# Swapping the partition halves of landmark sums by DMA instead of folding them on TensorE, with a new start and new schedule constants

## Chip, cores, metric

One core of one Trainium2 chip. The metric is the device time of one execution in microseconds (us), the slowest core's. Executions of one kernel mostly agree within 0.3%, though here runs of the kernel before lie between 252.5 and 256.1 us. Every comparison below is therefore with runs of the kernel before on the same chip, in the same rounds.

A ratio is the mean time of one kernel's fast runs over the mean time of the other's fast runs of the same rounds, so it isn't quite the ratio of the medians that are quoted. "Span" is the time from the first to the last instruction in a profiled run, some 1.7 to 2.1 us less than that run's time. "First MLP matmul" is always the first product of group `ps<-AT,G`, and not the product with w_in that comes before it.

## The reference

Nyström attention on 8 batches, 8 heads, 576 tokens, head size 64, then an MLP with squared relu. Landmarks are means of 18 neighbouring tokens of q and of k; 32 for each head.

```python
q_lm = q.reshape(B, H, m, S // m, D).mean(axis=3)      # m = 32
k_lm = k.reshape(B, H, m, S // m, D).mean(axis=3)
A  = sm(q, k_lm);  Bm = sm(q_lm, k_lm);  C = sm(q_lm, k)
Z = Bm.T / (norm1(Bm) * norm_inf(Bm) + 1e-06)
for _ in range(6):
    Z = 2 * Z - Z @ Bm @ Z
x = (A @ Z @ C @ v)             # heads side by side: (4608, 512)
g = np.maximum(x @ moe_w_in, 0.0) ** 2                  # (4608, 2048)
out = g @ moe_w_out
```

## The kernel before

A list scheduler inside the kernel (`Plan`) orders all operations when the program is built. It has a cost for each operation and a table of small moves (`SHIFTS`, one byte for each operation), searched offline for exactly this list of operations. On the chip each engine then runs its operations in that fixed order and waits where data is late.

The code cuts of this document are shortened. For batches 2 to 7 VectorE makes the landmark sums from the transposed q and k. The transposed tiles hold the 64 head dimensions of even tokens in one half of the partitions and those of odd tokens in the other, so each landmark is split into two partial sums, one in each half. A matmul with a fold matrix adds the halves, and the result has to come out of PSUM again:

```python
# attention(b), sums by VectorE
s1: t1 = T[:, :, 0, :] + T[:, :, 1, :]
s2: t2 = t1 + T[:, :, 2, :]
s3: part = reduce_sum(t2)                      # 128 partitions x 256, two halves to be added
...
def fold_mm(e, part=part, fp=fp):
    t = bank(fp, [P, H, M])
    nc.tensor.matmul(t.rearrange("p h m -> p (h m)"), lhsT=fold[:], rhs=part, start=True, stop=True)
...
if nm == "k":
    add(either(256), ... copy(e, kdup[:], PS[fp][:]), reads=[fp], writes=["kdup"])
else:
    for i in range(2):
        add(either(256), ... copy(e, bdq[64 * i:64 * i + 64, :, i, :], PS[fp][64 * i:64 * i + 64, :, :]), ...)

def b_mm(e):                                   # the landmark product, first user of kdup
    ...
    nc.tensor.matmul(t[:, i, :], lhsT=qpad[:, P * h:P * h + P], rhs=kdup[:, h, :], ...)
```

The start of batch 0: half of k comes in f32 through SyncE's queue and is cast by the engines, half by GpSimd's casting load. TensorE warms up with 46 zero matmuls, then transposes k in two groups of 12 chunks.

```python
def stage_k(e):
    nc.sync.dma_start(kst..., k[0, 0:H // 2]...)
...
load("k", 0, 2, (1,))                          # heads 4 to 7, casting
...
n = 12 if first else 6                         # chunks in a group of transposes
fill = {("k", 0): 46, ("q", 0): 3}.get((nm, x0), 0) if first else 0
```

The next batch's input loads are issued by GpSimd as soon as the transposes of the batch at hand have landed: a copy of one element of `qT` to `gate` makes GpSimd wait for them.

The softmax here doesn't subtract the row's maximum and nothing guards it: scores larger than these inputs give would overflow.

## Time and profile before

| | before |
|---|---|
| median of three runs | 254.35 us (254.19 to 254.66) |
| span of the profiled run, a fourth one of 253.56 us | 251.9 us |
| TensorE busy from 30 to 248 us | 214.92 of 218 us |
| first matmul of the MLP | 23.14 us |

The landmark product, first user of the folded sums, in the groups of instructions; the columns are line, engine, operation, tiles, sizes and count, then busy time in us and mean ns, then idle time before them with what ended it:

```profile
L707 PE MATMUL ps<-kdup,qpad 128*128 128x32 bf16 x56 | 2.5, 176 | 0.0
```

TensorE waits 0.0 us for it: kdup is always there in time. Two stretches in which the changed kernel will turn out differently (length, then PE, PEld, DVE, ACT, POOL, granted clock, DMA share, GB/s):

```profile
65.00:70.00 5.00, 4.95 (x56) 3.06 (x55) 4.22 (x14) 3.98 (x9) 0.00 (x0) 1.00 1.12 201
92.00:102.00 10.00, 9.79 (x129) 5.95 (x130) 9.12 (x34) 7.46 (x13) 0.18 (x1) 1.00 0.88 152
```

TensorE is full in both, at full clock.

### The profile page before, as it was taken

The page shows a single profiled execution, that of the slowest core. Times are in us where ns is not written, and L with a number is a line of the kernel's source. Part 1 is how long each engine was busy: PE and PEld are TensorE (multiplying, and loading weights), DVE is VectorE, ACT ScalarE, POOL GpSimd, SP SyncE. Part 2 cuts the span into 40 slices and gives each one's busy share as a digit, 9 for nine tenths or more (in the row PEclk, how much of TensorE's full clock was granted, in tenths as well). Part 3 has the DMA queues.
Part 4 walks back from the last instruction along what each step waited for, and adds up shares of the span by engine and source line. Part 5 has one row for each costly group of instructions (what it writes and reads, how often), then busy time and mean ns, then how long its engine had stood idle before and what let it go on. Part 6 is the DMA issues. An engine that isn't in the chain of part 4 may idle for free.

```text
span 251.9 us, 6505 instructions
## 1 busy us (share of the span) xinstructions
PE 240.2 (95%) x2621; PEld 144.5 (57%) x2658; DVE 173.1 (69%) x479; ACT 164.7 (65%) x287; POOL 28.9 (11%) x51
## 2 busy tenths in 40 slices
PE   7887999999999999999999999999999999999993
PEld 7563874557554665466646565556544664466453
DVE  3664887869874999499698797987932756477000
ACT  3386898068773997487879977667814873388021
POOL 7822200004004000300220003001000000000000
PEclk9997999999999999999999999999999999999999
DMA  7999999999998999799599778999222203211123
GB/s 151 186 204 205 205 206 205 189 180 159 217 168 165 187 178 183 109 215 158 119 151 249 135 149 111 222 174 162 72 61 75 57 18 86 61 34 32 42 83 85
DMA packets 57054, 35.58 MB, mean 141 GB/s; under 512 B 29760, under 2 KB 52544, under 8 KB 57024
## 3 DMA queue, kind: packets, MB, share of 16 engines
q0 software_dynamic: 22672, 18.06, 48.0%
q1 hardware_dynamic: 34352, 17.11, 32.3%
q8 instruction: 20, 0.33, 0.5%
q14 instruction: 10, 0.08, 0.1%
HBM read 36.70 MB, written 9.44 MB: 183 GB/s over the span
## 4 chain that ended last, share of the span: by engine, by line
PE 84%; DMA 6%; issue 2%; POOL 2%; ACT 2%; DVE 1%; SPq 0%; ACTq 0%; POOLq 0%; DVEq 0%
PE ps L1179 47%; PE ps L380 13%; PE ps L1123 12%; DMA vraw<-in_v_dram 4%; PE ps L1061 3%; DMA out_dram<-o 3%; PE ps L917 2%; PE ps L966 1%; PE ps L869 1%; PE ps L899 1%; PE ps L1006 1%; PE ps L681 1%; POOL qraw L456 1%; DVE gT L1138 1%; PE ps L948 0%
## 5 line engine op out<-in xcount | busy, mean ns | idle before, releaser
L1179 PE MATMUL ps<-w_out_bf,gT 128*128 128x512 bf16 (+1 forms) x557 | 137.7, 373 | 2.1 <-issue 1.0
L1135 ACT ACTIVATE r<-ps 128x576 bf16<-128x576 f32 x128 | 76.5, 661 | 12.1 <-PE ps L380 10.5
L1179 PEld LDWEIGHTS <-gT 128*128 128x128 bf16 x592 | 53.5, 98 | 46.2 <-issue 5.7
L1138 DVE TENSOR_TENSOR gT<-r 128x576 bf16<-128x576 bf16 x128 | 55.9, 454 | 17.5 <-PE ps L1179 8.6
L1123 PE MATMUL ps<-AT,G 128*128 128x288 bf16 x256 | 66.5, 288 | 0.4
L380 PE MATMUL ps<-AT,G 128*128 128x288 bf16 x256 | 66.5, 288 | 0.0
L388 ACT COPY o<-ps 128x512 f32<-128x512 f32 (+1 forms) x30 | 17.1, 572 | 42.0 <-PE ps L1179 35.6
L380 PEld LDWEIGHTS <-G 128*128 128x128 bf16 x256 | 25.2, 98 | 10.6 <-issue 0.2
L1123 PEld LDWEIGHTS <-G 128*128 128x128 bf16 x256 | 25.2, 98 | 9.8 <-ACT G L388 0.8
L388 ACT CAST G<-ps 128x1024 bf16<-128x1024 f32 (+2 forms) x22 | 19.5, 940 | 5.2 <-PE ps L1061 5.1
L390 DVE CAST G<-ps 128x1024 bf16<-128x1024 f32 (+2 forms) x14 | 14.9, 1070 | 8.3 <-PE ps L1061 8.1
L882 DVE SCALAR_TENSOR_TENSOR st<-st,ps 128x128 bf16<-128x128 bf16 x35 | 10.0, 286 | 10.8 <-PE ps L869 10.7
L553 POOL COPY gate<-qT 1x1 bf16<-1x1 bf16 x6 | 1.6, 274 | 126.6 <-DMA qT<-qraw 107.6
L924 ACT ACTIVATE EC<-ps 96x512 bf16<-96x512 f32 x24 | 13.2, 605 | 0.5 <-PE ps L917 0.5
L532 DVE TENSOR_TENSOR Pd<-st,ones_d 128x256 bf16<-128x256 bf16 x42 | 12.2, 290 | 0.9
L869 PEld LDWEIGHTS <-Pd 128*128 128x128 bf16 x84 | 7.8, 97 | 8.5 <-DVE Pd L532 1.7
L1011 ACT ACTIVATE Ra<-ps 128x576 f32<-128x576 f32 x16 | 10.4, 655 | 3.5 <-PE ps L380 3.3
L1022 DVE TENSOR_TENSOR AT<-Ea,Ra 128x576 bf16<-128x576 bf16 x16 | 11.8, 753 | 0.3 <-ACT Ra L1015 0.3
L999 ACT ACTIVATE Ea<-ps 128x576 bf16<-128x576 f32 x16 | 9.8, 653 | 2.6 <-PE ps L899 2.5
L1061 PE MATMUL ps<-w_in_bf,WT 64*32 64x512 bf16 (+1 forms) x264 | 10.6, 390 | 0.0
L560 PE MATMUL ps<-zeros 128*128 128x128 bf16 (+2 forms) x51 | 6.2, 295 | 2.5 <-DVE zeros L482 1.3
L917 PEld LDWEIGHTS <-kT 128*128 128x128 bf16 x192 | 7.3, 98 | 2.0 <-DMA out_dram<-o 0.6
(156 smaller groups left out, 247.8 us busy)
## 6 DMA issues: line engine op xcount, KB each, us to landing
vraw<-in_v_dram POOLq DMA_DIRECT2D x8, 576.0 KB, 7.9
out_dram<-o SPq DMA_DIRECT2D x23, 192.0 KB, 2.7
qraw<-in_q_dram POOLq DMA_DIRECT2D x7, 576.0 KB, 13.4
kraw<-in_k_dram POOLq DMA_DIRECT2D x7, 576.0 KB, 11.0
out_dram<-o SPq DMA_DIRECT2D x24, 128.0 KB, 2.4
w_in_bf<-in_moe_w_in_dram POOLq DMA_DIRECT2D x4, 512.0 KB, 14.7
w_out_bf<-in_moe_w_out_dram POOLq DMA_DIRECT2D x4, 512.0 KB, 21.0
out_dram<-o SPq DMA_DIRECT2D x23, 64.0 KB, 2.6
```

The costliest lines, as they stand in the source:

```text
L380: nc.tensor.add_instruction(mybir.InstMatmult(start_tensor_calc=start, stop_tensor_calc=stop, is_transpose=transpose, ldweights=False, til ...
L388: nc.scalar.copy(dst, src)
L390: ENG[e].tensor_copy(dst, src)
L532: nc.vector.tensor_tensor(dst[:], src.unsqueeze(2).to_broadcast([P, 2, NG, M]), ones_d[:].unsqueeze(1).to_broadcast([P, 2, NG, M]), ALU.mult)
L917: nc.tensor.matmul(t[:, y, :], lhsT=Ts["k"][z][:, o:o + P], rhs=flat(bdq[:, h, :, :]), start=True, stop=True)
L924: nc.scalar.activation(EC[:, x, :, :, :, :].rearrange("p c i g m -> p (i g) c m"), PS[sc][0:TP, :, :].rearrange("p y (c m) -> p y c m", c= ...
L1022: add(("DVE", dve_ns(S)), lambda e, i=i: nc.vector.tensor_tensor(AT[:, i, :], Ea[:, i, :, :].rearrange("p c t -> p (c t)"), Ra[:, i, :, :] ...
L1061: nc.tensor.matmul(ts[i][M * g:M * g + M, lo:hi], lhsT=WT[64 * i:64 * i + 64, g, :], rhs=w_in_bf[64 * i:64 * i + 64, g, n * 512 + lo:n * 5 ...
L1123: (again if j else nc.tensor.matmul)(t[:, j, 0:HALF], lhsT=G[:, i, f * P:(f + 1) * P], rhs=AT[:, i, j * HALF:(j + 1) * HALF], start=(i == ...
L1135: add(("ACT", act_ns(S)), lambda e, hk=hk, r=r: nc.scalar.activation(r.rearrange("p (j t) -> p j t", j=2), PS[hk][:, :, 0:HALF], AF.Relu), ...
L1138: add(("DVE", dve_ns(S, 2)), lambda e, r=r, f=f: nc.vector.tensor_tensor(gT[:, f, z * S:z * S + S], r[:], r[:], ALU.mult), reads=[("r", rn ...
L1179: nc.tensor.matmul(PS[ok][:, 0:hi - lo], lhsT=gT[:, f, x0:x0 + P], rhs=w_out_bf[:, f, lo:hi], start=(f == f0), stop=(f == f1 - 1))
```

## The change

The intent is to take 12 fold matmuls and 18 PSUM evictions off the engines. A DMA by SyncE copies each half of the partial sums into the other half of a second tile, and VectorE adds the two tiles in bf16. Beside that the start is changed (two heads of k in f32, six by the casting load, finer transposes, more filling matmuls), and the scheduler gets other constants for loads and instruction fetch, with a new table of moves. The core of the diff (the table, declarations and repeated lines cut):

```diff
-LOADS = {11: 1.0, 12: -1.0, 14: 1.0, 15: -1.0, 20: 2.0, 22: -2.0}
+LOADS = {11: 1.0, 12: -1.0, 13: 1.0, 14: -1.0, 21: 1.0, 22: -1.0}
 SHIFTS = ( ... )                                   # new table, cut
-    DMA_NS_PER_BYTE = 1.0 / 410.0
+    DMA_NS_PER_BYTE = 1.0 / 401.0
-    ... FETCH = 256, 67, ((20000.0, 6000.0), ...
+    ... FETCH = 256, 67, ((22000.0, 6400.0), ...
+            if op.dma < 0:
+                op.fin = op.end + op.land
-                op.fin = dma_free + (650.0 if op.lead > 0 else 4500.0)
+                op.fin = dma_free + op.land         # 1200 for loads; first k and q loads times 1.11
...
+    qpart = sb.tile([P, NG, 2, M], BF16, name="qpart")
+    swaps = {nm: sb.tile([P, NG, 2, M], BF16, name=nm + "sw") for nm in ("k", "q")}
-    kst = sb.tile([TP, H // 2, NC6 * D], F32, name="kst")
+    kst = sb.tile([TP, 2, NC6 * D], F32, name="kst")
...
-                n = 12 if first else 6
+                n = 6 if fine else 12               # fine: all but q of batch 0
-                    fill = {("k", 0): 46, ("q", 0): 3}...
+                    fill = {("k", 0): 60, ("q", 0): 3}...
+                        if n == 6:
+                            idle(bank(tp, [P, 512]))   # up to 8 zero matmuls before the second group of k
...
+            if b > 1:
+                def swap(e, part=raw_part[nm], sw=swaps[nm]):
+                    for x in range(2):
+                        nc.sync.dma_start(sw[64 * x:64 * x + 64], part[64 - 64 * x:P - 64 * x])
+
+                add(("SP", 120.0), swap, ..., dma=-1.0, prio=-40.0 + b, land=3500.0)
+                if nm == "k":
+                    add(("DVE", ...), ... tensor_tensor(kdup..., parts["k"][:], swaps["k"][:], ALU.add), ...)
+                else:
+                    add({"POOL": 500.0}, ... tensor_copy(parts["q"], qpart[:]), ... writes=["qpad"])
+                    for i in range(2):
+                        add(("DVE", ...), ... tensor_tensor(bdq[r, :, i, :]..., qpart[r], swaps["q"][r], ALU.add), ...)
+                continue
...
-            cuts = [(0, 256), (256, 512)] if last else [(0, 512)]
+            cuts = [(0, 384), (384, 512)] if last else [(0, 512)]
...
-                          k[0, 0:H // 2]...
+                          k[0, 0:2]...
-    load("k", 0, 2, (1,))
+    add(("POOL", 475.0), lambda e: nc.gpsimd.dma_start(raws["k"][0][:, 2:H], k[0, 2:H]...), ...)
```

`land=3500.0`: the scheduler assumes that a swap lands 3.5 us after its issue.

## The prediction

> **What bounds the kernel now.** I read the page's first two parts, then busy time by stretches, then the chain that ended last in order of time, then the TensorE timeline around the operations that the change takes away, then the transfers. Page, busy time and the clock of 40 slices:
>
> ```profile
> PE 240.2 (95%) x2621; PEld 144.5 (57%) x2658; DVE 173.1 (69%) x479; ACT 164.7 (65%) x287; POOL 28.9 (11%) x51
> ...
> PEclk9997999999999999999999999999999999999999
> ...
> q8 instruction: 20, 0.33, 0.5%
> ```
>
> Busy time by stretches (length, then PE, PEld, DVE, ACT, POOL, granted clock, DMA share, GB/s):
>
> ```profile
> 0.00:10.00 10.00, 8.13 (x121) 7.07 (x122) 5.22 (x23) 2.67 (x5) 8.50 (x21) 1.00 0.90 161
> 10.00:20.00 10.00, 7.98 (x229) 5.48 (x230) 5.69 (x29) 7.87 (x19) 3.99 (x6) 1.00 1.27 202
> 20.00:30.00 10.00, 9.13 (x133) 6.18 (x134) 6.59 (x16) 7.35 (x16) 2.52 (x4) 0.83 1.27 206
> 30.00:248.00 218.00, 214.92 (x2144) 125.80 (x2175) 155.63 (x413) 146.44 (x250) 13.92 (x22) 1.00 0.77 136
> ```
>
> From 30 to 248 us TensorE is busy 214.92 of 218 us. There time is saved only by giving TensorE less to do, or by removing part of 3.1 us of gaps. The rest is the start (the first matmul of the MLP is issued at 23.14 us) and the tail. The start, from the chain in order of time (start, length, what):
>
> ```profile
> 6.61 9.83 DMA vraw<-in_v_dram
> 16.48 1.19 PE ps L948 x24
> ...
> 18.98 0.24 DVE Z4T L983
> 19.26 0.32 PE ps L560
> 19.98 0.75 issue
> ...
> 130.80 6.52 DMA out_dram<-o
> ```
>
> The first batch's v lands at 16.44 us; from it a fixed chain runs to the MLP. In that chain 0.75 us is "issue", in the middle of one group of equal small matmuls, so no data was awaited. The clock was 0.83 on average between 20 and 30 us: one stretch of 3.4 us at half speed (the row of stretches for 22.00 to 25.40 has 0.50). MLP matmuls of 288 columns are 0.24 us apart there, 0.12 us later.
>
> The operation that the change removes, in the TensorE timeline:
>
> ```profile
> 32.28 0.27 PE L681 MATMUL ps<-kpart,fold 128*128 128x256 bf16 x1
> 32.38 0.27 PE L681 MATMUL ps<-qpad,fold 128*128 128x256 bf16 x1
> 32.49 0.29 PE L1123 MATMUL ps<-AT,G 128*128 128x288 bf16 x1
> ```
>
> Starts are 0.10 and 0.11 us apart: this, not the 0.27 us of its length, is what a fold costs a saturated TensorE.
>
> **What the Trainium skill says.** "TensorE: Matmul & The Clock Gate", section Back-to-back issue gap, gives N/2.4 + 2.5 ns warm, 109 ns for 256 columns; the trace agrees (0.21 us for two). The same page, "The HAM clock gate", tells of half speed for a window of some 3.4 us after too little activity; the trace agrees, with one such window in mid-run. "Runtime: NRT & Kernel Launch", section Instruction fetch mechanics: instructions come in blocks of 16 KiB, 256 instructions, at a cost that is mostly hidden. The trace has 20 such packets of 16 KB, and one is not hidden: the 0.75 us above. "DMA: Bandwidth & Descriptors", section Queues, rings and completion order, says that an engine goes round between its queues a packet at a time. The trace is harsher on a late comer: with input loads in flight a store takes 5 to 7.7 us to land, against 2.0 to 2.4 us when it is alone.
>
> **The change part by part.**
>
> 1. Folds. Landmark sums lie as partial sums in two halves of the partitions; a matmul with a fold matrix added the halves. For the six batches 2 to 7 both folds (k, q) go: 12 x 0.108 us = 1.3 us off TensorE, in its saturated stretch. Batches 0 and 1 keep theirs. With them go 6 k evictions (386 ns ACT or 421 ns DVE) and 12 q evictions (368 or 421 ns). In their place: 24 transfers of 32 KB by SyncE, 18 bf16 additions on VectorE, and 6 copies on GpSimd (sums into the padded q). An addition of 256 columns in bf16 should take what the mask multiplication of that size takes in the group list, 290 ns. Per batch VectorE gets 3 x 0.29 = 0.87 us and loses about half of three evictions, 0.6 us: +0.3 us; ScalarE loses about 0.6 us. Neither bounds the whole, so no gain beyond the 1.3 us.
>
> 2. The wait in its place. A swap issued alone should land after 2.0 to 2.3 us. But the next batch's loads are issued as soon as q's transpose lands: 57.4 us for v, the last landing near 70 us. VectorE ends the k sums at 60.97 us and the q sums at 65.47 us, in the midst of it. From the stores in that state I estimate 4.5 to 5.5 us for a swap; the plan in the code allows 3.5. In the changed program's order VectorE does the whole of the q sums, some squares and other work between the k sums and the k addition: 7 squares x 0.45 + 2 x 0.55 + 0.95 = 5.2 us in batch 2, 3.9 us in batch 3. So the k swap is nearly hidden. Between the q sums and the q additions lie 3.4 to 4.6 us of work, plus the landmark exponential in some batches: VectorE may stand for 0 to 1.5 us per batch. Four buffers between ScalarE and VectorE and three score banks pass little of that to TensorE: I book 0.4 us in all.
>
> 3. Mode switches. Going between full and split array costs about 0.09 us in the trace (0.309 us instead of 0.216 between a 512-column matmul and the next kind). In the built order after the first MLP matmul there are 58 such switches before and 55 after: 0.3 us less.
>
> 4. The start. SyncE now brings 2 heads of k in f32 instead of 4, GpSimd's cast load 6 instead of 4. The f32 part had landed at 5.14 us and should land near 3.8. But source bytes ahead of v are the same 4.6 MB and the DMA engines have been busy from 2 us on, so v lands at 16.4 to 16.8 us as before. The warm-up goes from 46 to 60 zero matmuls plus 7 of 512 columns between the k groups. They add rows to the instruction stream: the fetch block that ran dry in the middle of the last small products (row 703 of TensorE's order) now begins in the product before, which the v chain needs. Blocks came 6.2 us apart (instruction packets at 11.95, 18.51 and 24.47 us), so it may be ready only at 20.3 to 20.9 us. I book +0.3 us for the start, and assume that the half-speed window stays.
>
> 5. w_in's second block now comes after k of batch 1, v of batch 1 before the last two of w_out: order only, needed later than they land. Finer k transposes for batch 0 shorten evictions that are not in the chain.
>
> 6. The tail. The last tile is cut 384/128 instead of 256/256. TensorE's work is equal, the last eviction is shorter by about 0.1 us, but the larger store is issued 0.9 us before the last and holds SyncE. I book 0.
>
> Sum: 254.35 - 1.3 - 0.3 + 0.4 + 0.3 = 253.45. The new plan is also said to use measured load times; of the 3.1 us of gaps some should go, for which I take 0.6 us off: 252.9 us.
>
> **The rivals.** (a) The swap becomes the wait. TensorE's order is fixed, so a late k or q addition stops it before the landmark product or the scores, up to 1.5 us in each of six batches: +5 to +9 us, 258 to 262 us. For it: the 6.52 us store in the chain, landings up to 7.7 us. Against: 4 to 5 us of VectorE work lie in between, and 32 KB is less than any store. (b) The start improves: if the fetch stall and the half-speed window both vanish, 0.75 + 1.1 us (2.26 us of MLP at half speed, halved) come off on top: 251 us. For it: the added fill is there to hold the clock. Against: the block boundary falls in a worse place. (c) VectorE becomes the bound where it is already busy 9.7 of 10 us (90 to 100 and 110 to 120 us): 0.3 us per batch becomes TensorE time, and the gain is half lost: 254.5 us. (d) The folds were hidden anyway and nothing moves: 254.3 us; the even spacing above speaks against it.
>
> **Range and chances.** Certain are 1.3 us of work removed; the other terms lie within about 2 us either way: 251.0 to 255.2 us. Faster by over 2% needs less than 249.3 us, that is 3.5 us more than the folds: 0.04. Slower by over 2% needs over 259.4 us, rival (a) almost in full: 0.03. Within 2%: 0.93.
>
> **What would show it.** Fold matmuls x4 instead of x16, TensorE's sum down by a little over 1 us between 30 and 248 us; swap landings with median 3 to 5 us and a waiting time of VectorE for them under 6 us in all; TensorE waiting for a swap or an addition nowhere over 1 us. First MLP matmul at 22.9 to 23.9 us, v landing within 0.4 us of 16.44, a half-speed window in the first 30 us. Wrong it would be if waits for the swapped tiles head the waits of VectorE with over 10 us, or if the first MLP matmul comes before 22 us.

## The result, and the profile after

The changed kernel takes 264.22 us in the median of four runs (262.1 to 264.67), the kernel before 254.27 us (252.84 to 254.66, four runs). The ratio of the fast runs is 1.0385, 95% interval 1.0316 to 1.0454: slower. The result passes the comparison with the reference. The prediction, 252.9 us with a range up to 255.2, was wrong. The profiled run is the quickest of the four (262.1 us, granted clock 0.987); the other three have 0.980.

The page of the changed kernel: busy time and clock.

```profile
PE 246.2 (95%) x2669; PEld 144.3 (55%) x2669; DVE 174.0 (67%) x492; ACT 161.4 (62%) x276; POOL 30.7 (12%) x57
...
PEclk9997999999999997999999999999999999999999
```

A second dip of the clock stands in slice 16 of 40. TensorE's busy sum can mislead here: a matmul at half clock is "busy" for longer. The same stretches as before:

```profile
20.00:30.00 10.00, 8.82 (x132) 5.03 (x132) 5.49 (x15) 6.33 (x15) 2.73 (x4) 0.83 1.27 206
65.00:70.00 5.00, 3.04 (x23) 1.85 (x22) 2.93 (x7) 2.54 (x5) 0.46 (x1) 1.00 1.30 218
92.00:102.00 10.00, 7.77 (x46) 4.34 (x45) 5.75 (x20) 4.54 (x8) 0.40 (x1) 0.83 1.25 222
```

TensorE loses 2 us in each of the last two, and in the last one the clock is at half speed for 3.4 us as well. What it waits for (engine, line, releaser: us in total, times, longest):

```profile
PE ps L739 <- DVE kdup L696: 4.2, 2, 2.2
PE ps L764 <- issue: 1.8, 1, 1.8
...
PE ps L739 <- ACT r L1167: 0.9, 1, 0.9
```

Line 739 is the landmark product, which never waited before. It stops TensorE three times: 1.96 us from 67.94, 2.21 us from 93.60, 0.90 us from 146.91. In the third the addition into kdup was done at 146.65 us, before TensorE stopped, and the swap reached TensorE by another way:

```profile
146.36 0.29 DVE L696 TENSOR_TENSOR kdup<-kpart,ksw 128x256 bf16<-128x256 bf16 x1 [2.11 <-DMA ksw<-kpart]
147.11 1.74 ACT L1167 ACTIVATE r<-ps 128x576 bf16<-128x576 f32 x3 [1.20 <-DVE gT L1170]
147.81 0.35 PE L739 MATMUL ps<-kdup,qpad 128*128 128x32 bf16 x8 [0.90 <-ACT r L1167]
```

VectorE had stood 2.11 us for the swap, so its next square came late; ScalarE's relu stood 1.20 us for that square, and TensorE 0.90 us for the relu. VectorE in batch 2, in order of time (start, length, instruction, idle time before it):

```profile
61.97 0.95 DVE L682 TENSOR_REDUCE kpart<-t 128x256 bf16<-128x768 bf16 x1
...
66.47 1.02 DVE L1170 TENSOR_TENSOR gT<-r 128x576 bf16<-128x576 bf16 x2
69.56 0.29 DVE L696 TENSOR_TENSOR kdup<-kpart,ksw 128x256 bf16<-128x256 bf16 x1 [2.07 <-DMA ksw<-kpart]
```

The k sums are ready at 62.92. SyncE issues the two transfers of the swap one after the other, at 62.94 and 63.48, and the second lands at 69.47. VectorE has work until 67.49 and then stands, because its next instruction is the addition. TensorE stands behind it until 69.91. The chain that ended last has the same transfer in batches 2 and 3 (and in batch 5), and the stall of the start (start, length, what):

```profile
19.38 1.80 issue
...
63.48 5.99 DMA ksw<-kpart
...
88.90 6.47 DMA ksw<-kpart
```

Issues and landings of the swaps (queue, count, KB each, median us to landing):

```profile
ksw<-kpart SPq DMA_DIRECT2D x12, 32.0 KB, 4.4
qsw<-qpart SPq DMA_DIRECT2D x12, 32.0 KB, 2.2
```

The median hides the shape. In the last batch, which loads nothing beside it, a swap lands 1.8 us after its issue. The swaps of k in batches 2 and 3 are issued 4 to 8 us after the input loads that follow in GpSimd's order (55.6 to 57.1 and 83.2 to 84.8 us) and land after 5.7 to 6.5 us.

At the start, TensorE between the first two groups of k, and the first matmul of the MLP:

```profile
7.53 0.38 PE L566 MATMUL ps<-zeros 128*128 128x512 bf16 x1 [0.72 <-ACT kT L391]
7.74 1.46 PE L383 MATMUL ps<-zeros 128*128 128x512 bf16 x6
9.03 0.18 PE L640 MATMUL ps<-seg,kraw 96*128 96x32 bf16 x1
...
26.30 0.29 PE L1155 MATMUL ps<-AT,G 128*128 128x288 bf16 x1
```

The filling zeros wait 0.72 us for a PSUM bank and then hold TensorE until 9.03 us, though the rest of k had landed at 8.0. The landmark product of batch 0 comes at 13.33 us (11.29 before), and the first MLP matmul at 26.30 (23.14 before). Some 0.4 us of that is no loss: a group of batch 1's k (25.88 to 26.30 at least) now stands ahead of it and came later before.

Another 1.1 us is no loss either: the kernel before ran its first MLP matmuls at half speed until 25.40 us (half of 2.26 us lost), while the half-speed window of the changed kernel, 21.73 to 25.15 us, was over before its MLP began.

The account by spans, 260.3 - 251.9 = 8.4 us: start +1.6 as an estimate (3.16 less 0.4 and 1.1), the three stops +5.1 (1.96 + 2.21 + 0.90), the second half-speed window (96.83 to 100.24 us) +1.7 as an estimate (half of its 3.4 us), the tail +0.8 (from the end of the last eviction to the end of the span 4.2 us, 3.4 us before; SyncE is still issuing stores then), the removed folds -1.3 and mode switches -0.3 as predicted, not measured. That gives 7.6; 0.8 us is left unassigned.

Why did the stop of batch 3 bring a half-speed window, and that of batch 2 none? "TensorE: Matmul & The Clock Gate", section The HAM clock gate, tells of a free-running window of 3413 ns. The trace agrees. The half-speed window began at 96.83, so the windows before it run from 93.42 to 96.83 and, seven windows of 3.413 us earlier, from 69.53 back to 66.11. The stop of batch 3 (93.60 to 95.81) lies wholly in one of them. Of the stop of batch 2 (67.94 to 69.91) 1.59 us lie in one window and 0.38 us in the next. Two of the later runs show the same: in start_no_gap_fill a stop of 2.71 us (68.56 to 71.27) lies in one window (68.52 to 71.93) and a half-speed window follows; in swap_by_pool a stop of 2.76 us (171.75 to 174.51) has 0.87 us in one window and 1.89 us in the next, and none follows. The same stop of 2 us costs 2 or nearly 4 us, depending on where it falls. In the three other runs the clock of 0.980 against 0.987 stands, as an estimate, for one more window: 0.007 x 260 = 1.8 us, about what they take longer (1.9 to 2.6 us).

### The profile page after: what moved, and what is told of

It is laid out like the page before. It is cut to its first block, busy times and chain, and to the rows that moved or that the text cites. A ratio compares the mean times of both kernels' runs of the same rounds, so it can differ in the third digit from the quotient of the medians.

```text
span 260.3 us, 6621 instructions
## 1 busy us (share of the span) xinstructions
PE 246.2 (95%) x2669; PEld 144.3 (55%) x2669; DVE 174.0 (67%) x492; ACT 161.4 (62%) x276; POOL 30.7 (12%) x57
## 4 chain that ended last, share of the span: by engine, by line
PE 82%; DMA 7%; DVE 6%; ACT 2%; issue 1%; SPq 0%; DVEq 0%; ACTq 0%
PE ps L1211 44%; PE ps L383 13%; PE ps L1155 9%; DMA ksw<-kpart 7%; PE ps L566 3%; PE ps L1093 3%; PE ps L949 2%; DVE gT L1170 2%; PE ps L998 1%; PE ps L901 1%; ACT r L1167 1%; DVE kpart L682 1%; PE ps L931 1%; PE ps L1038 1%; PE ps L739 1%
## 5 line engine op out<-in xcount | busy, mean ns | idle before, releaser
L1211 PE MATMUL ps<-w_out_bf,gT 128*128 128x512 bf16 (+2 forms) x592 | 145.5, 375 | 0.0
L1211 PEld LDWEIGHTS <-gT 128*128 128x128 bf16 x592 | 52.8, 98 | 47.2 <-issue 5.9
L391 ACT COPY o<-ps 128x512 f32<-128x512 f32 (+2 forms) x30 | 17.1, 573 | 35.3 <-PE ps L1211 35.0
L383 PEld LDWEIGHTS <-G 128*128 128x128 bf16 x256 | 25.2, 99 | 11.3 <-issue 0.7
L1155 PEld LDWEIGHTS <-G 128*128 128x128 bf16 x256 | 25.2, 99 | 10.7 <-ACT G L391 0.7
L700 POOL COPY qpad<-qpart 128x256 bf16<-128x256 bf16 x6 | 2.5, 423 | 70.0 <-DVE qpart L682 48.5
L566 PE MATMUL ps<-zeros 128*128 128x128 bf16 (+2 forms) x67 | 8.2, 286 | 2.1 <-DVE zeros L488 1.3
```

What stands on the lines that cost most here:

```text
L383: nc.tensor.add_instruction(mybir.InstMatmult(start_tensor_calc=start, stop_tensor_calc=stop, is_transpose=transpose, ldweights=False, til ...
L391: nc.scalar.copy(dst, src)
L566: (again if x and not pairs else nc.tensor.matmul)(t, lhsT=zeros[:, 0:P], rhs=zeros[:, 0:t.shape[1]], start=True, stop=True, skip_group_ch ...
L1155: (again if j else nc.tensor.matmul)(t[:, j, 0:HALF], lhsT=G[:, i, f * P:(f + 1) * P], rhs=AT[:, i, j * HALF:(j + 1) * HALF], start=(i == ...
L1211: nc.tensor.matmul(PS[ok][:, 0:hi - lo], lhsT=gT[:, f, x0:x0 + P], rhs=w_out_bf[:, f, lo:hi], start=(f == f0), stop=(f == f1 - 1))
```

## The experiments

Theory A at this point: the swap's landing under load is the loss, in stops and the clock window behind them, and the changed start is the rest. Rivals: VectorE has become the bound; TensorE's new order is bad in itself; the start is all of it. Twelve kernels ran, in three sessions with one chip each (kernel before: 254.9, 253.57 and 253.49 us median).

| run | what | median us (runs) | ratio to before, 95% interval |
|---|---|---|---|
| swap_unread | additions don't read the swapped tiles | 254.48 (4) | 1.0013, 0.9966 to 1.0060 |
| folds_back | folds on TensorE again, rest of the change kept | 258.45 (4) | 1.0171, 1.0123 to 1.0218 |
| start_lean | 46 warming matmuls, no zeros between k groups | 259.81 (4) | 1.0119, 1.0026 to 1.0212 |
| land_6500 | scheduler expects the swap after 6.5 us | 260.54 (4) | 1.0257, 1.0202 to 1.0312 |
| swap_by_dve | swap by VectorE copies | 257.62 (6) | 1.0145, 1.0108 to 1.0183 |
| swap_by_pool | swap by GpSimd copies | 261.83 (4) | 1.0300, 1.0233 to 1.0367 |
| start_no_gap_fill | no zeros between k groups | 263.65 (4) | 1.0379, 1.0332 to 1.0426 |
| dve_no_gap | VectorE copies and no zeros | 257.12 (4) | 1.0120, 1.0070 to 1.0169 |
| before_start_retuned | kernel before with the new start alone | 255.50 (4) | 1.0073, 1.0037 to 1.0109 |
| land65_retuned | expects 6.5 us, table of moves searched again | 255.66 (4) | 1.0073, 1.0032 to 1.0114 |
| old_start_land65 | the same, with the start of before | 252.69 (6) | 0.9969, 0.9928 to 1.0010 |
| old_start_act | start of before, swap by ScalarE copies, searched again | 254.12 (6) | 1.0013, 0.9983 to 1.0043 |

### The wait taken away: swap_unread

```diff
-  tensor_tensor(kdup..., parts["k"][:], swaps["k"][:], ALU.add)
+  tensor_tensor(kdup..., parts["k"][:], parts["k"][:], ALU.add)
-  tensor_tensor(bdq..., qpart[r], swaps["q"][r], ALU.add)
+  tensor_tensor(bdq..., qpart[r], qpart[r], ALU.add)
```

The swaps are still issued and move the same bytes; every engine keeps its order. The sums are wrong on purpose (one half doubled), which the comparison with the reference doesn't notice: it calls this run correct too. So a passed comparison is weak evidence for the landmark sums of any run here.

> The changed kernel with one edit: the three additions per batch read the landmark sums twice and not the swapped copy (the result is wrong on purpose). Order of all engines, swap transfers and VectorE's work stay, only the wait for the swaps' landing goes. Theory S (late swaps stop TensorE before the landmark product, 2.1 + 2.4 + 1.1 us in the trace, and the idle time brings half-speed windows of 1.7 us each): 255.5 to 258 us, no TensorE gap over 0.5 us after 30 us, clock 0.99. Rival V (VectorE's added work and the new order of loads cost it): stays at 262 to 264.5 us.

Measured: 254.48 us, 1.0013. The waits of TensorE that are left, and the landing of the swaps that nobody waits for:

```profile
PE ps L764 <- issue: 1.8, 1, 1.8
...
ksw<-kpart SPq DMA_DIRECT2D x12, 32.0 KB, 6.0
```

No wait before line 739 is left, and the late start is still there (issue 1.8, first MLP product at 27.39). The time is even 1 us under the range expected. The landings are even longer, 6.0 us in the median. So it is the waiting for the transfer, not its bytes and not TensorE's order, that costs some 3.7% (1.0385 against 1.0013). Theory A stands; "the start is all of it" falls.

### The folds again, and a leaner start: folds_back, start_lean

folds_back puts fold matmuls and evictions back for all batches and keeps the rest of the change:

```diff
-            if b > 1:      # swap
+            if b > B:      # never
-                acq=(("o", fp),), ...
+                acq=(("o" if first else "n", fp),), ...
```

> The changed kernel with TensorE folds and evictions in place of the swaps for batches 2 to 7 too (an empty entry keeps the plan's table aligned); the start, the loads' order and the tail stay changed. Theory S with a start that costs about 3 us: before 254.3 + 3.2 = 257 to 258.5 us, TensorE stops of over 1 us after 30 us gone. Rival V or a loss from the re-tuned plan: 260 us or more. If the start costs nothing outside the profiled run: 254.5 us.

Measured: 258.45 us, 1.0171. No stop of TensorE over 0.4 us is left after 30 us, so the swap is needed for the stops. But the table of moves was searched for another list of operations, and the kernel's own plan ends 3.4 us later than that of the changed kernel. What the folds are worth can't be read from this run.

start_lean takes 14 warming matmuls and the zeros between the k groups out, when instructions are emitted; the order stays:

```diff
-  warm(t[:, 0:P] if pairs else t, fill, pairs)
+  warm(t[:, 0:P] if pairs else t, min(fill, 46), pairs)
-  if n == 6: idle(bank(tp, [P, 512]))
+  if n == 6: pass
```

> The changed kernel with 46 instead of 60 warm-up matmuls at the beginning and none of the seven 512-column ones between the k groups; the order of all else is the same. Theory F (the added zero matmuls hold TensorE from the second k group, whose data had landed at 8.0 us, to 9.0 us and push the landmark product of batch 0 from 11.3 to 13.3 us): first MLP matmul 1 to 2.5 us earlier than 26.3 us, total 1 to 2.5 us less than the changed kernel, 261.5 to 263 us. Rival D (the start is late because k and q land later, 8.0 and 10.98 us against 7.13 and 10.33): 0 to 0.6 us less. Rival H (the warm-up was needed, the clock falls to half earlier): slower than the changed kernel.

Measured: 256.07 to 262.37 us, and the profile fell in a slow run. Its first MLP product comes at 25.80, 0.5 us earlier than in the changed kernel (1 to 2.5 us expected), and it lists no issue wait at the start, so with fewer instructions the fetch stall is gone. But TensorE then stood 1.7 us for k, and a half-speed window from 8.23 to 11.64 us took its place. It is too scattered to say more.

### What the scheduler believed: land_6500, land65_retuned

```diff
-  dma=-1.0, prio=-40.0 + b, land=3500.0)
+  dma=-1.0, prio=-40.0 + b, land=6500.0)
```

> The changed kernel with the plan told that a swap lands after 6.5 us instead of 3.5 us; right result, another order on all engines. Theory S: TensorE has other work while the swaps are under way, the stops before the landmark product fall under 0.5 us each, and the time is near that of the kernel whose additions do not read the swaps: 255.5 to 259 us. If the stops are not from the landing (rival V): 262 us or more. The table of shifts was tuned for another plan, so up to 1.5 us of loss would be of the order alone.

Measured: 260.54 us, 1.0257, above the 255.5 to 259 us expected. No stop before the landmark product is left, but the order has new stops (0.5 us before line 1065 and 0.7 us before line 1093 around 86 us, more around 111 us). Its own plan ended 6.6 us later than that of the change: the old table of moves doesn't suit the new figure. So I gave the scheduler 6.5 us (2.2 us in the last batch) and searched the table again, with random moves kept if its own plan got shorter, until it ended as early as that of the change (245.4 us in its own count).

> The changed kernel with the landing of the swap DMA set to 6.5 us in the plan (2.2 us in the last batch, which loads nothing beside it) and the table of moves searched again, so that its own plan ends as early as that of the changed kernel did with 3.5 us. Swap, start and folds are those of the change. If the loss in the middle is only that the plan didn't expect the landing, and the wait can be hidden: no stop before the landmark product over 0.5 us, one half-speed window, 254.5 to 257, what is left being the start. If the wait can't be hidden (the earlier run with 6.5 us and the table of the change took 260.5 us): 259 or more.

Measured: 255.66 us, 1.0073. TensorE's three longest waits in this run, and the swap's landing:

```profile
PE ps L764 <- issue: 1.7, 1, 1.7
PE ps L1211 <- issue: 1.4, 9, 0.2
PE ps L566 <- DVE zeros L488: 1.3, 1, 1.3
...
DMA to landing us min/median/max: 1.8/5.2/6.3
```

The transfers are as slow as before, and nobody but VectorE waits for them (2.0 us in two places). The run reads the swapped tiles, and its start, swaps and folds are those of the change: 3.1 of its 3.85% came from a plan made for a landing time of 3.5 us that is 4.1 to 6.5 us on the chip for the k swaps of batches 2, 3 and 5 (1.0385 less 1.0073). A new search that keeps the 3.5 us was not run, so what the search alone gives is not shown; its plan was no shorter than that of the change.

### A swap without a DMA: swap_by_dve, swap_by_pool, old_start_act

```diff
-  nc.sync.dma_start(sw[64 * x:64 * x + 64], part[64 - 64 * x:P - 64 * x])
+  nc.vector.tensor_copy(sw[64 * x:64 * x + 64], part[64 - 64 * x:P - 64 * x])    # or nc.gpsimd
```

VectorE can write other partitions than it reads: "Vector Engine (DVE) Microarchitecture Reference", section The reshape front-end and per-opcode configuration, gives two possible target halves for an operation on 33 to 64 partitions. No run here shows it beyond doubt: the variants with VectorE, GpSimd and ScalarE all pass the comparison, but so did the wrong sums of swap_unread.

> The changed kernel with each swap made by two VectorE copies across the partition halves (64x256, bf16) instead of two DMAs, at the same place in the program; TensorE, ScalarE and GpSimd keep their order, the result is exact. Theory (the swap DMA lands 5 to 6.5 us after its issue while input loads are in flight, and that wait with the clock window behind it is the loss): the stops before the landmark product (2.13, 2.37, 1.06 us) go, the second half-speed window goes, span near that of the run whose additions did not read the swapped tiles (253.5 us), time 253.5 to 256. Rival 1 (VectorE is the bound, it has no room for 24 more copies of some 0.2 us, 5 us in all): time stays over 258. Rival 2 (the stops come from the order of TensorE's work, not from the DMA): stops before the landmark product stay, over 260.

> The same swap by two GpSimd copies instead. In GpSimd's order the swap of k now stands before the input loads of the next batch, so these loads start some 7 us later (at about 63 us instead of 55.6 for batch 2) and no DMA swap is left. Theory: no stop before the landmark product, 254 to 256 if the later loads have slack; if they have none, new stops behind the transposes of the next batch and 256 to 260. Rival (the DMA swap is not the cause): over 261.

Measured: 257.62 us (1.0145) by VectorE and 261.83 us (1.0300) by GpSimd. VectorE's copies and what is left of the wait:

```profile
L691 DVE COPY qsw<-qpart 64x256 bf16<-64x256 bf16 x12 | 3.4, 284 | 0.3
L691 DVE COPY ksw<-kpart 64x256 bf16<-64x256 bf16 x12 | 2.7, 222 | 0.3
...
PE ps L739 <- DVE kdup L696: 0.9, 2, 0.7
```

The swap is done 0.5 us after the sums, and 2.4 of the 3.85% are back. VectorE pays 6.1 us for it, and part of that reaches TensorE: 1.3% more than with no wait and no copies at all. So VectorE's time is not free, but it isn't the bound: my expected 253.5 to 256 us was too low by 1.6 us, rival 1's "over 258" too high.

GpSimd's copies take 530 to 560 ns and bring another wait:

```profile
L691 POOL COPY ksw<-kpart 64x256 bf16<-64x256 bf16 x12 | 6.7, 560 | 119.6 <-DVE kpart L682 119.4
...
PE ps L949 <- DVE bdq L704: 4.5, 3, 2.8
PE ps L739 <- POOL qpad L700: 2.1, 2, 1.7
```

GpSimd also issues the input loads, and in its order the copy of k stands ahead of them. So it waits for the sums (119.4 us of idle time, mostly of no cost) and the loads start late; I had expected 256 to 260 us for that case, and rivals named over 261. The cost is no longer the swap's landing but what stands behind the copy in GpSimd's order. That part of the reason is argued from the waits, not tried alone.

### The start: start_no_gap_fill, dve_no_gap, before_start_retuned

start_no_gap_fill is start_lean's second edit alone.

> The changed kernel without the seven zero products between the first two groups of k chunks (60 warming ones kept). If these products, which wait for a bank and then hold TensorE from 7.5 to 9.0 us, set the start: the second group of k starts when k has landed (about 8.1), first MLP product at 25.2 to 25.5 instead of 26.3, time about 1 us less, 263. If the clock falls to half speed in the gap instead (as in the run with 46 warming products): no gain, 264. If the start was lost in the loads alone: no change.

> Both: swaps by VectorE copies and no zero products between the first k groups. If the two add up: about 1 us under the VectorE swap alone, 252.5 to 255.

Measured: 263.65 us and 257.12 us, so no gain in the first, and 0.5 us, which the intervals don't separate, in the second (252.5 to 255 us was expected). In start_no_gap_fill the landmark product of batch 0 comes 5.57 us after the first product of k instead of 7.10, so the zeros did hold TensorE by 1.5 us. But this run has a half-speed clock from 20.73 to 27.56, two windows in a row, and its first MLP product comes at 26.86 us (25.2 to 25.5 expected):

```profile
20.00:30.00 10.00, 8.32 (x109) 4.58 (x110) 4.61 (x12) 5.56 (x13) 2.80 (x4) 0.66 1.27 206
```

What the earlier chain gains, the clock takes again. The cause isn't the zeros alone.

before_start_retuned puts the new start alone into the kernel before (loads of k, four groups, 60 warming matmuls, zeros), with entries for the five new operations in the table, which was searched again.

> The kernel before with one part of the change alone: the start (two heads of k by SyncE in f32 and six by the casting load, k in four groups of 6 chunks instead of two of 12, 60 warming products and up to 7 zero products between the groups); folds on TensorE, loads, constants and tail as before. The table of moves has entries inserted for the five new operations and was searched again, so that its own plan ends within 0.4 us of the plan of before. If the start of the change costs 2.6 to 3.2 us on its own: first MLP product at 25.5 to 26.3 instead of 23.1, time 256 to 257.5. If that loss comes from the changed load and fetch constants of the plan, which this kernel doesn't have: at most 255.

Measured: 255.50 us, 1.0073, between the two expectations. Its longest wait, and the stretch after it:

```profile
PE ps L736 <- issue: 1.7, 1, 1.7
...
20.00:30.00 10.00, 9.39 (x131) 6.03 (x132) 5.86 (x16) 7.47 (x17) 2.50 (x4) 0.71 1.27 206
```

The first MLP product comes at 25.13, 2.0 us later than in the profile of before; 0.6 us of that is a group of batch 1's q (from 24.50) that now stands ahead of it. The wait for instructions is 1.7 us instead of 0.75, and two half-speed windows follow each other (18.99 to 25.81). So the new start by itself costs through the fetch stall and the clock behind it. All profiled kernels with 60 warming matmuls have a stall of 1.7 to 2.0 us there; the three with 46 in other starts, and the kernel before, have 0.9 us or less. That the stall is instruction fetch is read from the traces: in all eleven profiles that have it, TensorE goes on 2.2 to 2.5 us after a 16 KB instruction packet starts (18.94 and 21.18 us in the changed kernel). In time the new start alone costs 1.9 us, of the 2.6 us that the next runs give to the start as a whole; the remaining 0.7 us may go with the plan's load constants, but the intervals don't separate the two figures. The plans point that way: the changed kernel's own plan puts the first MLP product at 22.29 us, that of the kernel before at 20.58, and that of this run at 20.69. The constants were not tried by themselves.

### The parts together: old_start_land65, old_start_act

Both have the start of the kernel before, with its load and fetch constants and its moves up to the second batch. The first keeps the DMA swap with 6.5 us, the second swaps by two ScalarE copies; both tables were searched again.

```diff
 # old_start_land65 against land65_retuned
-    kst = sb.tile([TP, 2, NC6 * D], F32, name="kst")
+    kst = sb.tile([TP, H // 2, NC6 * D], F32, name="kst")
-    fine = not first or nm == "k"
+    fine = not first
-    fill = {("k", 0): 60, ...
+    fill = {("k", 0): 46, ...
-    DMA_NS_PER_BYTE = 1.0 / 401.0;  FETCH = ((22000.0, 6400.0), ...;  land=1200.0
+    DMA_NS_PER_BYTE = 1.0 / 410.0;  FETCH = ((20000.0, 6000.0), ...;  land=650.0
 # old_start_act has, instead of the DMA
+    nc.scalar.copy(sw[64 * x:64 * x + 64], part[64 - 64 * x:P - 64 * x])
```

> The same, with the start of the kernel before (four heads of k by SyncE, two groups of 12 chunks, 46 warming products, its load and fetch constants, its moves up to the second batch). If start and unhidden swap are the whole of the loss and the folds are worth 1.3 us: 252 to 254, the same as before or up to 1% faster. If the swap costs in another way (more DMA, more DVE waits): 256 or more.

> The start of the kernel before, and each swap by two ScalarE copies across the partition halves instead of DMAs, planned as such (some 0.76 us a swap), table searched again. ScalarE is busy 62% of the time. If a swap without a DMA and without VectorE work is free: 252 to 254. If ScalarE's 24 copies of some 0.38 us (9 us in all) push out its exponentials and relus: 255 to 258.

Measured: 252.69 us, 0.9969, and 254.12 us, 1.0013; both as the theory has it. The page of old_start_land65 (busy time and clock; this profiled run has a span of 250.3 us):

```profile
PE 237.2 (95%) x2608; PEld 142.1 (57%) x2646; DVE 174.7 (70%) x491; ACT 160.5 (64%) x275; POOL 30.9 (12%) x57
...
PEclk9999999999999999999999999999999999999998
```

Against land65_retuned, whose swap and folds are the same, the start is worth 1.0073 / 0.9969 = 1.0104, that is 2.6 us. That is 1 us more than the account by spans has (1.6), and part of it is clock: the profile of land65_retuned has two half-speed windows there (23.42 to 30.25 us), that of old_start_land65 none. Against the kernel before, what is left of the change is 0.31% or 0.8 us gained, with an interval that reaches past zero. That agrees with 1.3 us for the folds and isn't a proof of it. It is the only version below the kernel before, and not by a margin that the runs settle. In old_start_act the copies take 403 ns, 24 of them 9.6 us of ScalarE, and the time is that of before.

The whole change then adds up: 3.85% is made of 3.1% for the plan's wrong landing time, 1.0% for the start, and -0.3% for the rest. swap_unread, on another chip, splits it otherwise: 3.7% for the wait leaves only 0.1% for start and rest together. The intervals of swap_unread and land65_retuned overlap, so the first split is good to about half a per cent.

## Why the prediction was wrong

1. **Folds, -1.3 us.** Right in kind: fold matmuls fall from 16 to 4 and TensorE keeps no wait for them. Their size is only bounded by the runs: 0.8 us gained for all that is left of the change, interval -1.8 to +0.3 us.

2. **The wait in its place, booked "0.4 us in all": this step failed, by its size.** Rival (a), given 0.03 with the range 258 to 262 us, is what happened, and a little more. It measured 5.1 us of stops and an estimated 1.7 us for the clock window behind them in the profiled run; taking the wait away was worth 3.7%. Three terms under it were off:
   - Landing: 4.5 to 5.5 us was estimated from the stores. In batches 2 and 3 the swap is two transfers issued 0.54 us apart, and the later one took 5.99 to 6.47 us; counted from the end of the sums, 6.5 to 7.0 us in batches 2 and 3.
   - Cover: 5.2 us of VectorE's work was counted for batch 2 and 3.9 for batch 3; measured 4.6 (62.92 to 67.49) and 3.9. By its own numbers the prediction had 0.6 to 1.6 us of wait in batch 3 and yet called the k swap "nearly hidden".
   - Passing on: "four buffers between ScalarE and VectorE and three score banks pass little of that to TensorE". In batches 2, 3 and 5 VectorE stood 2.07, 3.22 and 2.11 us and TensorE 1.96, 2.21 and 0.90: two thirds passed on. In batches 2 and 3 the next instruction in TensorE's fixed order was the user of the late tile itself; no buffer lies between those two. In batch 5 the buffers were in the way, and passed on 0.90 of the 2.11 us.

   The prediction also looked at the wrong swap: it allowed VectorE 0 to 1.5 us a batch behind the q swap, and in the trace no addition of q waits for one. Its own sign of being wrong, VectorE waiting over 10 us for the swaps, didn't show: it waited 7.6 us, in four places. The bound of 1 us on any wait of TensorE did (2.21 us).

   The clock was not in the step at all. A stop of 2 us can take a half-speed window with it.

3. **Mode switches, -0.3 us.** Not contradicted; too small to be seen in any run.

4. **The start, booked +0.3 us: this step failed too, by its size; 1.6 us by spans, 2.6 us between runs.** The longer fetch stall was foreseen ("it may be ready only at 20.3 to 20.9 us"); it ended at 21.18. The half-speed window stayed, as assumed (the prediction calls that of the kernel before "mid-run"; it stands in the start, at 21.99 to 25.40 us). What was missed is that the chain had slack only while v's landing bound it: the landmark product of batch 0 came 2.0 us later behind the zeros and the later k, so the product with v came at 17.99 instead of 16.48 us though v had landed at 16.45, as predicted. Both delays then lie in one chain. The scheduler's "measured load times", for which 0.6 us was taken off, may have cost time instead: its plan starts the MLP 1.7 us later than that of before, while the plan of before_start_retuned, with the old constants, starts it only 0.1 us later.

5. **Order of loads, 0**: nothing in the traces contradicts it; no run tried it alone.

6. **The tail, booked 0**: 0.8 us longer in the profile. The prediction named what could do it (the larger store "holds SyncE"); but land65_retuned, with the same cut of the last tile, has 3.4 us there like the kernel before, so the cut alone is not the cause, which stays open.

Rivals (b) and (d) are excluded, the first by the late start in all profiled kernels with the change's start, the second by TensorE's stops. Rival (c), VectorE as the bound, has the 1.3% of swap_by_dve for it when 6.1 us of copies are added, and nothing in the change itself.

Still open: why the swap waits for 3.5 to 4.5 us behind loads on another queue, and how much of the start's 2.6 us belongs to the plan's load constants rather than to its instructions. Of the account by spans 0.8 us is open.

## What to carry to other kernels

When an operation of a saturated engine is replaced by a transfer, ask what that transfer lands in, at the time when it is issued and counted to its last piece, not what it takes alone; then count, instance by instance, the work that covers it, and look at who uses the result next on the saturated engine, since buffers elsewhere don't help that one. A static schedule turns an optimistic latency into stops: here the right number and a new search gave back 3.1 of 3.85%. And judge a removed instruction by what it cost: 1.3 us of back-to-back matmuls was the whole prize, which any new wait of 0.2 us a batch would have eaten.

## What the Trainium skill lacked or had wrong

- "DMA: Bandwidth & Descriptors", section Queues, rings and completion order: it has the alternation between queues, but no figure for a small transfer on one queue while another queue has large loads under way. Measured for 32 KB between partitions: 1.8 us in the last batch, which loads nothing beside it, and 5.4 to 6.8 us for the other swaps of k when nobody waits for them (swap_unread).
- "Runtime: NRT & Kernel Launch", section Instruction fetch mechanics: the cost of a block boundary is called mostly hidden. It was 0.75 us in the kernel before and 1.7 to 2.0 us in every profiled kernel with 60 warming matmuls at the start, on the chain that sets the first MLP matmul.
- "TensorE: Matmul & The Clock Gate", section The HAM clock gate: the free-running window is right, and the page could add what follows from it: a stop of 2.2 us inside one window (93.60 to 95.81) cost a half-speed window of 3.4 us, a stop of 1.96 us across two (67.94 to 69.91) cost none, nor did one of 2.76 us across two in swap_by_pool.
- "Vector Engine (DVE) Microarchitecture Reference", section The reshape front-end and per-opcode configuration, has the write to the other partition half for VectorE without a duration: 222 to 284 ns for 64x256 in bf16. Such a copy by ScalarE (403 ns) or GpSimd (530 to 560 ns) I found on no page; the runs give its duration, and their comparison is too weak to prove where it writes.
